# Grouped-query decode attention with a small MLP on one core: another place for the turn of p and for the loads of wo

## The chip, the cores and the metric

The kernel runs on one core of a Trainium2 chip. It is one program with five instruction streams: PE (TensorE, matrix products), DVE (VectorE), ACT (ScalarE), POOL (GpSimd) and SP (SyncE, which issues nearly all loads). The metric is the device time of one execution in microseconds. Lower is better.

## The reference

One token is decoded. Its normalised activations `xn` go through two blocks whose results are added to the input. Block A is attention of 32 query heads over 4 cached key/value heads of 65,536 positions. Block B is a small MLP.

```python
B, Sq, D = 1, 1, 1024
Hq, Hkv, Sk, Dh = 32, 4, 65536, 128          # everything in bfloat16

xn = layernorm(A_x)
# A
q = (xn @ wq).reshape(B, Sq, Hq, Dh).transpose(0, 2, 1, 3)
k = repeat(k_cache, 8, axis=1); v = repeat(v_cache, 8, axis=1)
p = softmax(einsum("bhqd,bhkd->bhqk", q, k) * Dh ** -0.5)
o = einsum("bhqk,bhkd->bhqd", p, v)
A = o.transpose(0, 2, 1, 3).reshape(B, Sq, Hq * Dh) @ wo      # wo: 4096 x 1024
# B (a fixed shift of column groups stands between w1 and w2; with one token it leaves zeros)
x1 = xn + shift(gelu(layernorm(xn) @ w1)) @ w2
Bm = x1 + gelu(layernorm(x1) @ w3) @ w4                       # w3: 1024 x 3584
out = A_x + A + Bm
```

Keys and values are 67 MB each, the weights 36 MB together; all are read once.

## The kernel before

**Order by hand.** Each engine has a queue object (`_Q`) to which the Python program appends instructions, and waits on semaphores where a buffer (`_B`) was last written or read by another engine. Every engine runs its queue strictly in the order in which the program appended it. Two lists set this order. `loads` is the order in which SP issues loads. `uses` is the order in which the loaded pieces are consumed; each use appends its instructions to PE, DVE and ACT. After each use `issue()` appends as many further loads as the ring has room for.

**The ring.** `slots_sb` has 8 slots of 16 KB in each of 128 partitions, so 2 MB each. Loads of keys, of values, of wq, w3 and the first one of w4 take an aligned pair of slots (`load2`, up to 4 MB); w1, w2, each quarter of wo and the last two of w4 take one slot (`load`, `load_pieces`). Slots are given out round robin. A load of a pair after a load of one slot skips the other slot of that pair (`room` rounds up to an even place). SP waits, load by load, until the earlier content of the slots has been read.

**Keys.** A head of 65,536 keys comes in four loads, and each load is used as two chunks (`use_k`, chunks `ch` 0 to 7 of a head). For a chunk DVE makes four 32x32-block transposes from the slot into `X` (line 512, two buffers by the chunk's parity), then takes the maximum of the scores of the chunk before (`max_k`, line 528), which ACT copies from PSUM to `S_sb` (line 529). PE makes the chunk's scores in 16 matmuls (line 521). So a key slot is free when DVE has transposed it.

**End of a head's keys.** `finish_head(h)` takes the maximum of the last chunk and of the head, and ACT makes the exponentials, four activations of 128 x 1024 elements into `p_sb` (line 539), with their sums in `lcol`.

**Turn of p.** `transpose_p(h)` turns `p_sb` into `pT_sb`: four times eight PE transposes (line 545) into one PSUM tile, and one ACT copy out of it (line 548). Each group of eight waits for the copy before.

**Values.** A value load is also used as two chunks (`use_v`, `n` 0 to 7), each 16 matmuls on PE against `pT_sb` into `OT_ps` (line 559). A value slot is free when PE has read it. After a head's last chunk `combine(h)` follows: ACT copies `OT_ps` (line 566), PE sums the parts (lines 567, 569), DVE divides and writes the head's eight columns of `oP_bf` (lines 572 to 576).

**wo.** `use_wo(h)` multiplies the head's quarter of wo by its columns of `oP_bf`, in 32 matmuls that accumulate into `M1_ps` with the MLP's parts (line 431, in `rows_mv`). Each matmul takes 32 columns as the stationary side, of which the first matters.

**Order around the change.** After the weights of the front come the four key loads of head 0. From then on a key load of head h and a value load of head h-1 alternate; the last four value loads have no keys between them. wo of head h-2 comes after the first value load while head h's keys run, wo of head 2 after the first of the last four value loads, wo of head 3 after the last. w4 closes the list. The turn of p of head h-1 is appended after the second chunk of head h; that of the last head stands before its first value chunk:

```python
                use_k(h, ch, ld)
                if ch == 1 and h > 0:
                    transpose_p(h - 1)
                if ch == NCH - 1:
                    finish_head(h)
```

Of the kernel before, what the change touches and what calls it, by code (L numbers as in the profile page):

```python
# [6 lines left out]
BF = mybir.dt.bfloat16  # L7
F32 = mybir.dt.float32
ACTF = mybir.ActivationFunctionType
ALU = mybir.AluOpType  # L10
# [85 lines left out]
def _op(q, fn, reads=(), writes=(), partial=False):  # L96
    _deps(q, reads, writes)
    ev = q.op(fn, True)
    _done(ev, reads, writes, partial)
    return ev  # L100
# [33 lines left out]
def bass_parallel_sum__gqa_block_cached__mixer_s_mlp__decode_kernel(  # L134
# [14 lines left out]
    P = 128  # L149
    D = A_x.shape[2]  # L150
    HKV, SK, DH = A_k_cache.shape[1], A_k_cache.shape[2], A_k_cache.shape[3]
# [4 lines left out]
    R = D // P  # L156
# [14 lines left out]
    with ExitStack() as es:  # L171
# [3 lines left out]
        def sb(name, shape, dt):  # L175
            return E(nc.sbuf_tensor(name, shape, dt))
# [4 lines left out]
        def sem(name):  # L181
            return E(nc.semaphore(name))
# [41 lines left out]
        cb_rL = sb("cb_rL", [P, 1], F32)  # L224
        cb_m = sb("cb_m", [P, 16, R], F32)
        cb_o = sb("cb_o", [P, R], F32)
        oP_bf = sb("oP_bf", [P, HKV * R + 32], BF)
        xr_bf = sb("xr_bf", [P, RW], BF)
        accr = sb("accr", [P, RW], F32)
        g_bf = sb("g_bf", [P, R + 32], BF)  # L230
# [15 lines left out]
        q_dve = _Q("dve", sem("c_dve"))  # L246
# [178 lines left out]
        def rows_mv(nkk, parts, st_fn, b_st, b_slot, b_out, first, last, k0=0):  # L425
            fns = []
            for kk in range(k0, k0 + nkk):
                for out_fn, mv_fn in parts:
                    for j in range(4):
                        fns.append(lambda e, kk=kk, j=j, out_fn=out_fn, mv_fn=mv_fn, st=(first and kk == k0), sp=(last and kk == k0 + nkk - 1):  # L430
                                   e.matmul(out_fn(j), st_fn(kk), mv_fn(kk, j), start=st, stop=sp, tile_position=(0, 32 * j), skip_group_check=True))  # L431
            _grp(q_pe, fns, reads=b_slot + [b_st], writes=b_out, partial=not first)
# [36 lines left out]
        def d_parts(view, c0):  # L469
            return [(lambda t: M1_ps[32 * t:32 * t + 32, c0:c0 + RW], lambda kk, t: view[:, kk * D + t * RW:kk * D + (t + 1) * RW])]  # L470
# [28 lines left out]

        def use_wo(h, ld):  # L500
            view, b = ld[0:2]
            rows_mv(R, d_parts(view, 0), lambda kk: oP_bf[:, h * R + kk:h * R + kk + 32], b_oP[h], b, [b_M1], False, False)

# [25 lines left out]
        def finish_head(h):  # L531
            max_k(NCH - 1)
            _op(q_dve, lambda e: e.reduce_max(mrow[:, 0:1], mcol[:, :], axis=AX.X), reads=[b_mcol], writes=[b_mrow])
            _op(q_dve, lambda e: e.tensor_tensor(out=Rm[:, :], in0=sel16[:, :], in1=mrow[:, 0:1].broadcast_to([P, 16]), op=ALU.mult),  # L534
                reads=[b_mrow, b_const], writes=[b_R])
            _op(q_pe, lambda e: e.matmul(M0_ps[:, 16:32], Lmat[:, :], Rm[:, :], start=True, stop=True), reads=[b_R, b_sel], writes=[b_M0])  # L536
            _op(q_dve, lambda e: e.tensor_reduce(out=brun[:, 0:1], in_=M0_ps[:, 16:32], axis=AX.X, op=ALU.min), reads=[b_M0], writes=[b_brun])
            for x in range(NB):
                _op(q_act, lambda e, x=x: e.activation(p_sb[:, :, :, :, x], S_sb[:, 2 * x:2 * x + 2, :].rearrange("p s (c i) -> p s c i", i=32),  # L539
                                                       ACTF.Exp, bias=brun[:, 0:1], scale=SCALE, accum_out=lcol[:, h % 2, x:x + 1]),  # L540
                    reads=[b_Ss[2 * x], b_Ss[2 * x + 1], b_brun], writes=[b_p, b_lcol[h % 2]], partial=x > 0)

        def transpose_p(h):
            for c8 in range(2 * CL // 8):
                _grp(q_pe, [lambda e, i=i, c=8 * c8 + i: e.transpose(out=PT_ps[:, i * P:(i + 1) * P],  # L545
                                                                    in_=p_sb[:, c // CL, c % CL, :, :].rearrange("p i h -> p (i h)"), identity=ident_bf[:])
                            for i in range(8)], reads=[b_p, b_const], writes=[b_PT])
                _op(q_act, lambda e, c8=c8: e.activation(pT_sb[:, :, 32 * c8:32 * c8 + 32, :].rearrange("p a x g -> p x a g"),  # L548
                                                         PT_ps[:, :].rearrange("p (x a g) -> p x a g", x=32, a=NA), ACTF.Copy),
                    reads=[b_PT], writes=[b_pT], partial=c8 > 0)  # L550
# [13 lines left out]
        def combine(h):  # L564
            _op(q_dve, lambda e: e.reduce_sum(Lacc[:, :], lcol[:, h % 2, :], axis=AX.X), reads=[b_lcol[h % 2]], writes=[b_Lacc])  # L565
            _op(q_act, lambda e: e.activation(O_acc[:, :], OT_ps[:, :], ACTF.Copy), reads=[b_OT], writes=[b_O])  # L566
            fns = [lambda e: e.matmul(M0_ps[:, 0:1], selL[:, :, :].rearrange("p g x -> p (g x)"), Lacc[:, :], start=True, stop=True)]  # L567
            for t in range(4):
                fns.append(lambda e, t=t: e.matmul(M0_ps[:, 256:384], selX[:, t, :, :].rearrange("p g x -> p (g x)"), O_acc[:, t * P:(t + 1) * P],  # L569
                                                   start=(t == 0), stop=(t == 3)))  # L570
            _grp(q_pe, fns, reads=[b_Lacc, b_O, b_sel], writes=[b_M0])
            _op(q_dve, lambda e: e.reciprocal(cb_rL[:, :], M0_ps[:, 0:1]), reads=[b_M0], writes=[b_cb])  # L572
            _op(q_dve, lambda e: e.tensor_tensor(out=cb_m[:, :, :], in0=M0_ps[:, 256:384].rearrange("p (x r) -> p x r", r=R),
                                                 in1=dmask[:, :].unsqueeze(2).broadcast_to([P, 16, R]), op=ALU.mult), reads=[b_M0, b_const], writes=[b_cb])
            _op(q_dve, lambda e: e.reduce_sum(cb_o[:, :], cb_m[:, :, :].rearrange("p x r -> p r x"), axis=AX.X), reads=[b_cb], writes=[b_cb])
            _op(q_dve, lambda e: e.tensor_scalar(out=oP_bf[:, h * R:(h + 1) * R], in0=cb_o[:, :], scalar1=cb_rL[:, 0:1], scalar2=None, op0=ALU.mult),
                reads=[b_cb], writes=[b_oP[h]])


        loads = [("wq", 0), ("wq", 1), ("w1",), ("w2",), ("w3", 0), ("w3", 1)]  # L580
        uses = [("wq", j) for j in range(4)] + [("w1",), ("w2",)] + [("w3", j) for j in range(4)]
        for h in range(HKV):
            for i in range(4):
                loads.append(("k", h, i))
                uses += [("k", h, 2 * i), ("k", h, 2 * i + 1)]
                if h > 0:
                    loads.append(("v", h - 1, i))
                    uses += [("v", h - 1, 2 * i), ("v", h - 1, 2 * i + 1)]
                if h > 1 and i == 0:
                    loads.append(("wo", h - 2))  # L590
                    uses.append(("wo", h - 2))
        for i in range(4):
            loads.append(("v", HKV - 1, i))
            uses += [("v", HKV - 1, 2 * i), ("v", HKV - 1, 2 * i + 1)]
            if i == 0:
                loads.append(("wo", HKV - 2))
                uses.append(("wo", HKV - 2))
        loads += [("wo", HKV - 1)] + [("w4", i) for i in (0, 2, 3)]
        uses += [("wo", HKV - 1)] + [("w4", i) for i in range(4)]

        layer_norm(xP, b_x, xn, xn_bf, b_xn, 0)
        _op(q_dve, lambda e: e.tensor_scalar(out=accr[:], in0=xr_bf[:], scalar1=ln_s[:, 1:2], scalar2=ln_s[:, 4:5], op0=ALU.add, op1=ALU.mult),
# [20 lines left out]
        for it in uses:  # L623
            ld = ready.pop(it)
            kind, args = it[0], it[1:]
            if kind == "wq":
                if args[0] == 3:
                    late_consts()
                    layer_norm(xn, b_xn, xn2, xn2_bf, b_xn2, 2)
                use_wq(args[0], ld)  # L630
            elif kind == "k":
                h, ch = args
                use_k(h, ch, ld)
                if ch == 1 and h > 0:
                    transpose_p(h - 1)
                if ch == NCH - 1:
                    finish_head(h)
            elif kind == "v":
                h, n = args
                if h == HKV - 1 and n == 0:  # L640
                    transpose_p(h)
                use_v(h, n, ld)
                if n == 2 * NA - 1:
                    combine(h)
            else:
                dict(w1=use_w1, w2=use_w2, w3=use_w3, wo=use_wo, w4=use_w4)[kind](*args, ld)
            for i in ([ld[2]] if it[0] != "w3" else [ld[2] // 2 * 2, ld[2] // 2 * 2 + 1]):
                taken[i] -= 1
            issue()
# [38 lines left out]
```

## Time and profile before

| | |
|---|---|
| Time, median of 3 runs | 409.18 us (407.23 to 410.07) |
| The profiled execution, its own time | 409.36 us |
| Its span, first to last instruction | 407.4 us |
| Busy: PE, DVE, ACT, POOL | 156.6, 187.8, 80.5, 7.5 us |
| Read from memory | 169.87 MB, 417 GB/s over the span |
| Mean granted PE clock | 0.618 of full |
| Key and value loads, median from issue to landing | 29.3 and 27.5 us |
| SP waits for DVE's key transposes | 186.4 us in 15 waits |
| SP waits for PE's value matmuls | 113.5 us in 15 waits |

The profile is one execution. Times are microseconds from the span's start. A timeline row shows start, duration, engine, line, operation, destination <- source, count, and in brackets how long the engine was idle before and what ended that. A row by stretch shows its bounds, its length, the busy time and the instruction count of PE, of PE's weight loads, of DVE, ACT and POOL, then PE's granted clock, the busy share of the 16 DMA engines, and GB/s. SP's long waits mean only that the ring is full; a load lands some 28 us after its issue since two or three others are ahead of it in the queue.

### The profile page before, as it was taken

What the parts mean: (1) busy time and instruction counts of PE and PEld (TensorE: products, weight loads), DVE (VectorE), ACT (ScalarE), POOL (GpSimd) and SP (SyncE); (2) the same over time, 40 slices, a digit from 0 to 9 for tenths busy, and PEclk for the clock granted to TensorE, in tenths of its full rate; (3) what the DMA queues carried; (4) which work ended last, traced back from release to release, by engine and by line L of the source; (5) the groups of instructions that cost most, each with busy time, mean ns of one, the idle gap of its engine ahead of it and who ended that gap; (6) DMA issues with size and microseconds to landing.
All of it is one profiled execution on the core that took longest, in us unless ns stands there. A gap on an engine that the chain in (4) does not pass through costs nothing.

```text
span 407.4 us, 3981 instructions
## 1 busy us (share of the span) xinstructions
PE 156.6 (38%) x1647; PEld 71.8 (18%) x1647; DVE 187.8 (46%) x264; ACT 80.5 (20%) x87; POOL 7.5 (2%) x38
## 2 busy tenths in 40 slices
PE   0273333333257050523470323325731515364445
PEld 0132111111023020102240111122410101231133
DVE  0255029999846364608481828054908183100010
ACT  1000000111861010390320101912300005630000
POOL 5000000000000000000000000000000000000000
PEclk9985655555567557565677565555575655569556
DMA  8999999999999999999999999999999999999994
GB/s 360 412 423 440 420 444 431 420 450 415 441 430 415 449 425 431 439 417 438 431 384 441 434 413 450 421 428 439 375 412 415 452 418 421 454 412 384 418 405 195
DMA packets 7377, 170.12 MB, mean 418 GB/s; under 512 B 952, under 2 KB 960, under 8 KB 1856
## 3 DMA queue, kind: packets, MB, share of 16 engines
q1 hardware_dynamic: 7208, 169.87, 97.7%
q8 instruction: 13, 0.21, 0.2%
q14 instruction: 4, 0.03, 0.0%
q10 hardware_dynamic: 152, 0.00, 0.0%
HBM read 169.87 MB, written 0.00 MB: 417 GB/s over the span
## 4 chain that ended last, share of the span: by engine, by line
DMA 68%; DVE 21%; PE 7%; issue 3%; SPq 1%; POOL 0%; ACTq 0%
DMA slots_sb<-in_A_k_cache_dram 51%; DVE X L512 18%; DMA slots_sb<-in_B_w_dram 7%; DMA slots_sb<-in_A_v_cache_dram 7%; DMA xr_bf<-in_A_x_dram 3%; PE OT_ps L559 3%; DVE mcol L528 2%; PE S_ps L431 2%; PE S_ps L521 1%; SPq L310 1%; PE M_ps L407 0%; PE M_ps L415 0%; PE M_ps L536 0%; POOL ln_s L419 0%; DVE Rm L534 0%
## 5 line engine op out<-in xcount | busy, mean ns | idle before, releaser
L512 DVE STREAM_TRANSPOSE X<-slots_sb 128x1024 f32<-128x1024 f32 x128 | 147.2, 1209 | 79.2 <-DMA slots_sb<-in_A_k_cache_dram 79.2
L521 PE MATMUL S_ps<-X,Yall 128*32 128x512 bf16 x512 | 56.1, 582 | 147.2 <-DVE X L512 147.2
L529 ACT ACTIVATE S_sb<-S_ps 128x512 f32<-128x512 f32 x32 | 19.2, 599 | 206.9 <-DVE mcol L528 206.9
L559 PE MATMUL OT_ps<-slots_sb,pT_sb 128*32 128x512 bf16 x512 | 47.3, 533 | 16.2 <-DMA slots_sb<-in_A_v_cache_dram 11.4
L521 PEld LDWEIGHTS S_ps<-X,Yall 128*32 128x32 bf16 x512 | 16.4, 121 | 181.9 <-DVE X L512 167.0
L539 ACT ACTIVATE p_sb<-S_sb,brun 128x1024 bf16<-128x1024 f32 x16 | 41.6, 2597 | 1.9 <-DVE Lacc L565 0.8
L572 DVE RECIPROCAL cb_rL<-M_ps 128x1 f32<-128x1 f32 x4 | 0.7, 168 | 73.9 <-PE M_ps L569 73.9
L559 PEld LDWEIGHTS OT_ps<-slots_sb,pT_sb 128*32 128x32 bf16 x512 | 17.8, 125 | 39.4 <-issue 22.8
L528 DVE TENSOR_REDUCE mcol<-S_ps 128x1 f32<-128x512 f32 x32 | 21.1, 658 | 7.1 <-PE S_ps L521 7.1
L548 ACT ACTIVATE pT_sb<-PT_ps 128x1024 bf16<-128x1024 bf16 x16 | 16.4, 1024 | 19.2 <-PE PT_ps L545 19.2
L545 PE MATMUL PT_ps<-ident_bf,p_sb 128*128 128x128 bf16 x128 | 14.1, 277 | 13.4 <-ACT pT_sb L548 13.4
L431 PE MATMUL S_ps<-slots_sb,xn_bf 128*32 128x512 bf16 (+1 forms) x128 | 12.7, 570 | 10.6 <-DMA slots_sb<-in_B_w_dram 9.2
L545 PEld LDWEIGHTS PT_ps<-ident_bf,p_sb 128*128 128x128 bf16 x128 | 10.6, 126 | 18.6 <-ACT pT_sb L548 16.0
L567 PE MATMUL M_ps<-Lacc,selL 128*128 128x1 f32 x8 | 2.2, 348 | 24.6 <-ACT O_acc L566 24.6
L443 ACT ACTIVATE ge_a<-ge_b 128x8 f32<-128x8 f32 (+1 forms) x2 | 0.4, 216 | 52.2 <-DVE ge_b L442 52.2
L435 DVE STREAM_TRANSPOSE X<-S_ps 128x512 f32<-128x512 f32 (+1 forms) x3 | 2.5, 847 | 14.3 <-PE S_ps L431 14.2
L431 PE MATMUL M_ps<-slots_sb,gh_bf 128*32 128x256 bf16 x112 | 5.9, 365 | 6.7 <-DMA slots_sb<-in_B_w_dram 6.7
L569 PE MATMUL M_ps<-O_acc,selX 128*128 128x128 f32 x32 | 8.2, 438 | 0.0
L431 PEld LDWEIGHTS S_ps<-slots_sb,xn_bf 128*32 128x32 bf16 x128 | 4.3, 133 | 17.0 <-DMA slots_sb<-in_B_w_dram 10.0
L569 PEld LDWEIGHTS M_ps<-O_acc,selX 128*128 128x128 f32 x32 | 7.3, 333 | 0.0
L651 DVE TENSOR_TENSOR fin<-accr,M_ps 128x256 bf16<-128x256 f32 x1 | 0.4, 422 | 14.6 <-PE M_ps L431 14.6
L566 ACT ACTIVATE O_acc<-OT_ps 128x512 f32<-128x512 f32 x4 | 2.5, 619 | 23.3 <-PE OT_ps L559 23.3
(90 smaller groups left out, 64.7 us busy)
## 6 DMA issues: line engine op xcount, KB each, us to landing
slots_sb<-in_A_k_cache_dram SPq DMA_DIRECT2D x16, 4096.0 KB, 29.3
slots_sb<-in_A_v_cache_dram SPq DMA_DIRECT2D x16, 4096.0 KB, 27.5
slots_sb<-in_A_wq_dram SPq DMA_DIRECT2D x2, 4096.0 KB, 16.7
slots_sb<-in_A_wo_dram SPq DMA_DIRECT2D x4, 2048.0 KB, 29.4
slots_sb<-in_B_w_dram SPq DMA_DIRECT2D x2, 3584.0 KB, 33.6
slots_sb<-in_B_w_dram SPq DMA_DIRECT2D x2, 2048.0 KB, 28.0
slots_sb<-in_B_w_dram SPq DMA_DIRECT2D x1, 4096.0 KB, 27.8
slots_sb<-in_B_w_dram SPq DMA_DIRECT2D x5, 512.0 KB, 27.2
```

Of the source, the lines that this page charges most:

```text
L310: ev = q_sp.dma(lambda e, dst=dst, src=src: e.dma_start(out=dst, in_=src), ch.sem, 16 * ch.n)
L431: e.matmul(out_fn(j), st_fn(kk), mv_fn(kk, j), start=st, stop=sp, tile_position=(0, 32 * j), skip_group_check=True))
L435: _op(q_dve, lambda e: e.transpose(out=X32[:, 1, c0:c0 + 32 * n], in_=src), reads=b_src, writes=[b_X[1][0]], partial=c0 > 0)
L512: _op(q_dve, lambda e, ix=ix: e.transpose(out=X32[:, m, 1024 * ix:1024 * (ix + 1)], in_=K32[:, 1024 * ix:1024 * (ix + 1)]), reads=b, write ...
L521: fns.append(lambda e, we=we, c_mid=c_mid, mv=mv: e.matmul(S_ps[bank][32 * c_mid:32 * c_mid + 32, :], Yall[:, h, we, :, :].rearrange("p a ...
L528: _op(q_dve, lambda e: e.reduce_max(mcol[:, ch:ch + 1], S_ps[bank][:, :], axis=AX.X), reads=[b_S[bank]], writes=[b_mcol], partial=ch > 0)
L529: _op(q_act, lambda e: e.activation(S_sb[:, ch, :], S_ps[bank][:, :], ACTF.Copy), reads=[b_S[bank], b_mcol], writes=[b_Ss[ch]])
L539: _op(q_act, lambda e, x=x: e.activation(p_sb[:, :, :, :, x], S_sb[:, 2 * x:2 * x + 2, :].rearrange("p s (c i) -> p s c i", i=32), ACTF.Ex ...
L545: _grp(q_pe, [lambda e, i=i, c=8 * c8 + i: e.transpose(out=PT_ps[:, i * P:(i + 1) * P], in_=p_sb[:, c // CL, c % CL, :, :].rearrange("p i ...
L548: _op(q_act, lambda e, c8=c8: e.activation(pT_sb[:, :, 32 * c8:32 * c8 + 32, :].rearrange("p a x g -> p x a g"), PT_ps[:, :].rearrange("p ...
L559: fns.append(lambda e, cl=cl, q4=q4, x0=x0: e.matmul(OT_ps[32 * q4:32 * q4 + 32, :], pT_sb[:, a, x0:x0 + 4, :].rearrange("p x g -> p (x g) ...
L569: fns.append(lambda e, t=t: e.matmul(M0_ps[:, 256:384], selX[:, t, :, :].rearrange("p g x -> p (g x)"), O_acc[:, t * P:(t + 1) * P], start ...
```

## The change

The two lists are built from one loop with a lag of five loads between keys and values, and wo is loaded in two pairs: wo of heads 0 and 1 after value load 8 (counted over all heads), wo of heads 2 and 3 after value load 15. The turn of p of heads 1 to 3 is appended directly after `combine` of the head in front; that of head 0 stays after the second chunk of head 1. `oP_bf` gets 32 spare columns for each head instead of 32 behind the last.

```diff
-        oP_bf = sb("oP_bf", [P, HKV * R + 32], BF)
+        oP_bf = sb("oP_bf", [P, HKV, R + 32], BF)
...
-            rows_mv(R, d_parts(view, 0), lambda kk: oP_bf[:, h * R + kk:h * R + kk + 32], b_oP[h], b, [b_M1], False, False)
+            rows_mv(R, d_parts(view, 0), lambda kk: oP_bf[:, h, kk:kk + 32], b_oP[h], b, [b_M1], False, False)
...
-            _op(q_dve, lambda e: e.tensor_scalar(out=oP_bf[:, h * R:(h + 1) * R], in0=cb_o[:, :], scalar1=cb_rL[:, 0:1], scalar2=None, op0=ALU.mult),
+            _op(q_dve, lambda e: e.tensor_scalar(out=oP_bf[:, h, 0:R], in0=cb_o[:, :], scalar1=cb_rL[:, 0:1], scalar2=None, op0=ALU.mult),
...
-        for h in range(HKV):
-            for i in range(4):
-                loads.append(("k", h, i))
-                uses += [("k", h, 2 * i), ("k", h, 2 * i + 1)]
-                if h > 0:
-                    loads.append(("v", h - 1, i))
-                    uses += [("v", h - 1, 2 * i), ("v", h - 1, 2 * i + 1)]
-                if h > 1 and i == 0:
-                    loads.append(("wo", h - 2))
-                    uses.append(("wo", h - 2))
-        for i in range(4):
-            loads.append(("v", HKV - 1, i))
-            uses += [("v", HKV - 1, 2 * i), ("v", HKV - 1, 2 * i + 1)]
-            if i == 0:
-                loads.append(("wo", HKV - 2))
-                uses.append(("wo", HKV - 2))
-        loads += [("wo", HKV - 1)] + [("w4", i) for i in (0, 2, 3)]
-        uses += [("wo", HKV - 1)] + [("w4", i) for i in range(4)]
+        LAG = 5
+        order = [("k", i) for i in range(LAG)]
+        for i in range(LAG, 4 * HKV):
+            order += [("v", i - LAG), ("k", i)]
+        order += [("v", i) for i in range(4 * HKV - LAG, 4 * HKV)]
+        for kind, i in order:
+            h, j = divmod(i, 4)
+            loads.append((kind, h, j))
+            uses += [(kind, h, 2 * j), (kind, h, 2 * j + 1)]
+            if kind == "v" and i in (8, 15):
+                for n in ((0, 1) if i == 8 else (2, 3)):
+                    loads.append(("wo", n))
+                    uses.append(("wo", n))
+        loads += [("w4", i) for i in (0, 2, 3)]
+        uses += [("w4", i) for i in range(4)]
...
                 use_k(h, ch, ld)
-                if ch == 1 and h > 0:
-                    transpose_p(h - 1)
                 if ch == NCH - 1:
                     finish_head(h)
+                if h == 1 and ch == 1:
+                    transpose_p(0)
             elif kind == "v":
                 h, n = args
-                if h == HKV - 1 and n == 0:
-                    transpose_p(h)
                 use_v(h, n, ld)
                 if n == 2 * NA - 1:
                     combine(h)
+                    if h < HKV - 1:
+                        transpose_p(h + 1)
```

## The prediction

> **What bounds the kernel now.** I read the page first, then transfer rates by stretch, then the timeline from 155 to 405 us. Loads are numbered through all heads, K0 to K15 and V0 to V15, 4 MB each. From the page:
>
> ```profile
> q1 hardware_dynamic: 7208, 169.87, 97.7%
> ...
> L572 DVE RECIPROCAL cb_rL<-M_ps 128x1 f32<-128x1 f32 x4 | 0.7, 168 | 73.9 <-PE M_ps L569 73.9
> ```
>
> The load queue is busy 97.7% of the span and the busiest engine, DVE, 46%: the loads are the bound, and only time in which the queue lacks work can be won. In the second line DVE idles 73.9 us before the four reciprocals of `combine`; that costs time only where it lets the queue run dry. Rates by stretch (last columns: PE's granted clock, DMA share, GB/s):
>
> ```profile
> 20.00:200.00 180.00, 68.99 (x676) 28.03 (x668) 107.41 (x159) 36.71 (x41) 1.10 (x2) 0.59 1.00 430
> 200.00:220.00 20.00, 10.22 (x147) 5.50 (x144) 10.30 (x10) 4.27 (x5) 0.00 (x0) 0.81 0.96 407
> 220.00:284.00 64.00, 21.85 (x185) 9.18 (x185) 32.55 (x38) 15.43 (x16) 0.00 (x0) 0.53 1.01 433
> 284.00:304.00 20.00, 11.05 (x149) 6.23 (x147) 10.42 (x10) 4.27 (x5) 0.00 (x0) 0.67 0.94 391
> 304.00:360.00 56.00, 19.24 (x163) 8.68 (x163) 22.99 (x30) 16.57 (x17) 0.00 (x0) 0.56 1.00 432
> 360.00:380.00 20.00, 9.11 (x136) 4.64 (x136) 0.00 (x0) 1.40 (x2) 0.00 (x0) 0.76 0.95 388
> ```
>
> Fed, the queue moves 431 GB/s (mean of the three long stretches). The three short ones fall behind: 20 x (24 + 40 + 43) / 431 = 5.0 us. These are the holes. The timeline shows the first two:
>
> ```profile
> 185.19 0.17 DVE L572 RECIPROCAL cb_rL<-M_ps 128x1 f32<-128x1 f32 x1 [13.68 <-PE M_ps L569]
> 186.27 9.12 DVE L512 STREAM_TRANSPOSE X<-slots_sb 128x1024 f32<-128x1024 f32 x8
> 195.48 0.33 SPq L295 DMA_DIRECT2D slots_sb<-in_A_v_cache_dram  x1
> 205.23 3.60 PE L559 MATMUL OT_ps<-slots_sb,pT_sb 128*32 128x512 bf16 x32 [1.21 <-ACT pT_sb L548]
> 208.93 0.33 SPq L295 DMA_DIRECT2D slots_sb<-in_A_k_cache_dram  x1
> 222.47 4.62 DVE L512 STREAM_TRANSPOSE X<-slots_sb 128x1024 f32<-128x1024 f32 x4 [10.25 <-DMA slots_sb<-in_A_k_cache_dram]
> 241.90 4.62 DVE L512 STREAM_TRANSPOSE X<-slots_sb 128x1024 f32<-128x1024 f32 x4 [9.13 <-DMA slots_sb<-in_A_k_cache_dram]
> ```
> ```profile
> 285.66 4.62 DVE L512 STREAM_TRANSPOSE X<-slots_sb 128x1024 f32<-128x1024 f32 x4 [5.72 <-DMA slots_sb<-in_A_k_cache_dram]
> 293.73 0.33 SPq L295 DMA_DIRECT2D slots_sb<-in_A_k_cache_dram  x1
> 306.65 4.62 DVE L512 STREAM_TRANSPOSE X<-slots_sb 128x1024 f32<-128x1024 f32 x4 [10.08 <-DMA slots_sb<-in_A_k_cache_dram]
> ```
>
> V5 is issued at 195.48, when DVE has read K8. K10 needs V4's slots; PE reads V4 at 205.23 to 208.83, after turning p, and SP issues K10 at 208.93, too late. The price stands in the landings, since DVE starts on keys the moment they land: K10 (222.47) to K11 (241.90) is 19.43 for two loads, 9.72 each; K9 (DVE starts on it at 201.92) to K10 is 20.55, so 1.12 were lost. The same at K14: K13 (285.66) to K14 is 20.99, so 1.56 lost. The third hole is V15's, issued at 366.73 when V12 has been read: PE starts on V14 at 371.41 and on V15 at 382.13, 10.72 for one load, 1.00 lost. Sum 3.68 us. It is less than 5.0 because the rate is a mean of 16 DMA engines and a landing is that of the last; the end of the kernel follows landings, so I take 3.7 and keep 5.0 as the upper end.
>
> **The change, part by part.** *Order of keys and values.* Written out, both lists read K0 to K4, V0, K5, V1, K6 and so on to K15, V11, V12 to V15. Nothing changes: cost 0, one answer. Only wo moves.
>
> *wo in pairs.* Before, each wo load takes one slot, and the next 4 MB load skips the other: for its time in the ring three pairs of slots hold data and one is half empty. wo0 follows V4 and wo1 V8, just where the head's end holds up the slots. After, wo0 and wo1 fill one pair behind V8, wo2 and wo3 one behind V15. Same bytes, same four DMAs. Around the first hole wo0's 2 MB (4.9 us at 431 GB/s) leave the queue, and every load inherits another slot: K9 takes K7's, V5 takes V3's (free at 174.8, when PE has read V3; SP issued K9 then), K10 takes K8's (free at 195.4), V6 takes V4's. K9 plus V5 are now in the queue long before K8 is read. K10's data must start when V5 has landed: before, at 222.47 - 1.12 - 9.72 = 211.6, so after at 211.6 - 4.9 = 206.7. It is issued at 195.5; allowing 2 us from issue to data (after 293.73 the rate recovers within that), 9 us are spare.
>
> *p turned behind the last values of the head in front.* For heads 1 and 2 the 32 transposes and four evictions come directly after `combine`, ahead of K8's and K12's score matmuls. One turn takes 281.34 to 290.03, 8.7 us at half clock (4 x (1.03 to 1.04 PE + 1.02 ACT + hand-overs)). It waits for p, whose last exponential ends at 182.1, and `combine`'s matmuls already wait for ACT behind that and end at 185.15: no new wait for p. Queued behind the turn on PE are K8's 32 matmuls, and DVE's maxima wait for those. The turn runs 185.2 to 193.9. K8's first scores, ready at 191.0, go 193.9 to 195.8 and its second, ready at 195.5, to 197.7; DVE's first maximum waits 0.5 us past 195.31, covered by the 5.95 us in which DVE waits for K9 at 201.92. DVE reads K8 whole before that maximum, so K8's slots come free at 195.4 as before. On ACT the evictions stand before copies of scores not yet made. V4 then runs 197.7 to 201.4 instead of 205.2 to 208.8, and V6, which inherits its slots, needs data only at 216.4: 13 us spare. Uncovered, the turn would cost 8.7 us a head; its cover is those spares. Head 0's turn stays (only the order of two ifs changes), and head 3's follows `combine(2)` directly before and after.
>
> *Heads 2 to 3.* The same: V9 waits for DVE's reading of K12 (279.45 before, some 6 us earlier after, since wo0 is no longer ahead of it and the first hole is gone), needed when K13 lands at about 284.5: 9 us spare. K14 waits for V8, V10 for wo1's use, each needed over 10 us later. The holes of 1.12 and 1.56 go.
>
> *Tail.* V15 now inherits V11's slots, free at 344.6, not V12's: its 1.00 goes. wo2 and wo3 wait for V12 (about 364 after); V15 lands at about 382.1 - 3.7 - 4.9 = 373.5, so with 2 us to start they have 7.5 us spare, the smallest of all. PE uses wo2 behind `combine(3)`: 3.6 us of V15's matmuls and some 5 of combining, while wo2, wo3 and 4 MB of w4 (19.5 us) still come. Behind w4 the order is as before: the end follows its last piece. SP still issues ten DMAs in a row here, and the rate is 336 from 368 to 372 and 393 from 372 to 376; if the burst itself slows the queue, the 1.00 may stay: lower end 2.7.
>
> *oP_bf.* 160 columns instead of 64 to clear on POOL: its memset of 64 columns took 0.14 us and that of 512 (permWE) 0.51, so +0.1, hidden because POOL's constants end near 7 us and x arrives at 15.2. Uncovered 0.1.
>
> **Two rules against the rows.** Full rate: 169.87 MB at 431 GB/s are 394.1 us of the 407.4. The Trainium skill ("DMA: Bandwidth & Descriptors", Where 436 GB/s comes from) puts the ceiling at 435 GB/s; by that figure alone the bytes take 390.3 us, an estimate, and the row stands 1% short of it, so no order of loads makes the fed queue faster. PE clock: turned at full clock eight transposes took 0.62 us (199.52), at half clock 1.03 (197.37). The skill ("TensorE: Matmul & The Clock Gate", What's actually happening) says that the array falls to half clock after an idle window of about 3.4 us; it speaks against the new place, behind some 8 us in which PE waited for ACT, and an estimate from the two rows is 4 x 0.41 = 1.6 us more on a turn. I use 8.7, the half-clock turn, so the sum is the same by the rule and by the row.
>
> **Sum.** Span 407.4 - 3.7 = 403.7. The profiled execution took 409.36, 1.96 around its span: 405.7. It lay 0.18 above the median of 409.18: 405.5 predicted.
>
> **The rivals.** *A, holes filled* (0.55): 405.5, its own range 404.2 (gain 5.0) to 406.5 (gain 2.7), with 0.8 us either way for the spread of runs (407.23 to 410.07). *B, more than the landings show* (0.19): the mean rate counts, 5.0, and K14 to K15's 1.56 (306.65 to 327.64 is 20.99 again, with K15 issued 32 us ahead, so no slot caused it) also goes: 409.2 - 6.6 = 402.6. Against it: nothing in the change touches that load. *C, holes only move* (0.19): the queue runs dry at another load, or wo's and w4's burst slows it, and 1 to 2 us are won: 407.7. For it: 388 GB/s beside the tail's burst; against it: spares of 7 us and up. *D, slower* (0.07): the turn stands in the keys' way. If K8's and K12's slots were free only after the turn (8.7 later) and one more chunk on DVE (5.1, for a full X), K10 would be issued at 195.5 + 13.8 = 209.3, its data 4.6 us late, twice: 9.2 lost, 3.7 won, 414.7. It decides from 9 us of delay; DVE's program order, reading both chunks before it waits, speaks against it.
>
> **Chances.** A change of 1% (4.1 us: below 405.1 or above 413.3) is about what can be told from none. A lies just above that border, so I put 0.22 of it on faster and 0.33 on same; B is faster, C same; D slower. Faster 0.41, same 0.52, slower 0.07. The range leaves out D, the half of B beyond its centre and the slow end of C: 402.6 to 408.6.
>
> **What will show it.** Rates of 428 and over in every 20 us stretch from 20 to 380; keys landing 19.4 apart throughout; V5, K10, V6 issued at least 7 us before the load ahead lands; on PE the 32 transposes between `combine` and K8's scores. Wrong: a stretch under 420 between 190 and 300 (D or C), or a full queue at a lower rate.

## The result, and the profile after

The changed kernel takes 405.28 us (median of 6 runs, 405.25 to 405.43), the kernel before beside it 409.62 (6 runs, 407.23 to 410.27). The ratio is 0.9905, 95% interval 0.9878 to 0.9931: 0.7 to 1.2% faster. The median is 0.2 us from the forecast. The profiled execution took 405.26 with a span of 403.3, where 403.7 was forecast. The spread of the runs fell too, from 3.0 to 0.2 us.

Page of the kernel after, the same two lines as before:

```profile
q1 hardware_dynamic: 7208, 169.87, 98.4%
...
L572 DVE RECIPROCAL cb_rL<-M_ps 128x1 f32<-128x1 f32 x4 | 0.7, 168 | 68.3 <-PE M_ps L569 68.3
```

DVE still idles nearly as long before the reciprocals; the load queue's share rose. The rates by stretch (last column GB/s):

```profile
20.00:200.00 180.00, 72.92 (x724) 31.65 (x716) 110.53 (x162) 39.87 (x44) 1.10 (x2) 0.59 1.00 430
200.00:220.00 20.00, 6.76 (x64) 2.43 (x64) 10.87 (x12) 1.20 (x2) 0.00 (x0) 0.61 1.00 431
220.00:284.00 64.00, 27.38 (x299) 13.96 (x299) 29.01 (x35) 18.54 (x19) 0.00 (x0) 0.63 1.00 430
284.00:304.00 20.00, 6.85 (x64) 2.47 (x64) 10.30 (x10) 1.20 (x2) 0.00 (x0) 0.59 1.00 433
304.00:360.00 56.00, 21.04 (x171) 10.05 (x171) 23.00 (x30) 17.81 (x18) 0.00 (x0) 0.56 1.00 432
360.00:380.00 20.00, 13.76 (x142) 6.77 (x146) 0.00 (x0) 0.60 (x1) 0.00 (x0) 0.67 0.99 422
```

The stretches that stood at 407, 391 and 388 stand at 431, 433 and 422. Timeline of the kernel after, around the former first hole:

```profile
184.82 1.06 PE L545 MATMUL PT_ps<-ident_bf,p_sb 128*128 128x128 bf16 x8
...
186.15 9.12 DVE L512 STREAM_TRANSPOSE X<-slots_sb 128x1024 f32<-128x1024 f32 x8
...
192.26 1.90 PE L521 MATMUL S_ps<-X,Yall 128*32 128x512 bf16 x16
...
195.36 0.33 SPq L295 DMA_DIRECT2D slots_sb<-in_A_k_cache_dram  x1
...
196.36 1.93 PE L559 MATMUL OT_ps<-slots_sb,pT_sb 128*32 128x512 bf16 x32
197.03 4.62 DVE L512 STREAM_TRANSPOSE X<-slots_sb 128x1024 f32<-128x1024 f32 x4 [1.18 <-DMA slots_sb<-in_A_k_cache_dram]
198.38 0.33 SPq L295 DMA_DIRECT2D slots_sb<-in_A_v_cache_dram  x1
...
216.47 4.62 DVE L512 STREAM_TRANSPOSE X<-slots_sb 128x1024 f32<-128x1024 f32 x4 [9.13 <-DMA slots_sb<-in_A_k_cache_dram]
```

The turn begins directly behind `combine`, in PE's former wait for DVE's transposes. K10 goes out when K8 has been read (195.36, before 208.93), V6 when V4 has been read (198.38), and K9 (197.03) to K10 (216.47) is 19.44. Further on:

```profile
285.59 4.62 DVE L512 STREAM_TRANSPOSE X<-slots_sb 128x1024 f32<-128x1024 f32 x4 [11.61 <-DMA slots_sb<-in_A_k_cache_dram]
...
305.02 4.62 DVE L512 STREAM_TRANSPOSE X<-slots_sb 128x1024 f32<-128x1024 f32 x4 [9.13 <-DMA slots_sb<-in_A_k_cache_dram]
...
324.44 4.62 DVE L512 STREAM_TRANSPOSE X<-slots_sb 128x1024 f32<-128x1024 f32 x4 [9.12 <-DMA slots_sb<-in_A_k_cache_dram]
...
362.47 1.60 SPq L286 DMA_DIRECT2D slots_sb<-in_A_wo_dram  x2
...
373.10 3.61 PE L559 MATMUL OT_ps<-slots_sb,pT_sb 128*32 128x512 bf16 x32 [5.35 <-DMA slots_sb<-in_A_v_cache_dram]
```

K13 to K14 is 19.43 (before 20.99), K14 to K15 19.42 (before 20.99), and wo2 and wo3 are issued at 362.5, over 10 us before V15 lands at 373.1. Two details differ from the forecast: K13 lands when it did before (285.59 against 285.66), though the first hole is gone; and K15's unexplained 1.56 is gone too. Both come up again below, with the instruction loads.

### The profile page after: what moved, and what is told of

Read it like the earlier page. It is cut to its first block, busy times and chain, and to the rows that moved or that the text cites. A ratio compares the mean times of both kernels' runs of the same rounds, so it can differ in the third digit from the quotient of the medians.

```text
span 403.3 us, 3981 instructions
## 1 busy us (share of the span) xinstructions
PE 159.8 (40%) x1647; PEld 74.1 (18%) x1647; DVE 187.9 (47%) x264; ACT 80.5 (20%) x87; POOL 7.6 (2%) x38
## 4 chain that ended last, share of the span: by engine, by line
DMA 64%; DVE 21%; PE 7%; ACT 4%; issue 3%; SPq 1%; POOL 0%; ACTq 0%
DMA slots_sb<-in_A_k_cache_dram 53%; DVE X L512 18%; DMA slots_sb<-in_B_w_dram 8%; DMA xr_bf<-in_A_x_dram 3%; ACT p_sb L539 3%; PE OT_ps L559 3%; DVE mcol L528 2%; PE S_ps L431 1%; ACT pT_sb L548 1%; PE PT_ps L545 1%; PE S_ps L521 1%; SPq L310 1%; PE M_ps L569 0%; PE M_ps L415 0%; PE M_ps L407 0%
## 5 line engine op out<-in xcount | busy, mean ns | idle before, releaser
L521 PE MATMUL S_ps<-X,Yall 128*32 128x512 bf16 x512 | 58.3, 601 | 142.3 <-DVE X L512 142.3
L559 PEld LDWEIGHTS OT_ps<-slots_sb,pT_sb 128*32 128x32 bf16 x512 | 19.5, 130 | 32.4 <-issue 23.4
L545 PE MATMUL PT_ps<-ident_bf,p_sb 128*128 128x128 bf16 x128 | 16.6, 311 | 13.4 <-ACT pT_sb L548 13.4
L545 PEld LDWEIGHTS PT_ps<-ident_bf,p_sb 128*128 128x128 bf16 x128 | 12.9, 143 | 17.6 <-ACT pT_sb L548 16.6
L567 PE MATMUL M_ps<-Lacc,selL 128*128 128x1 f32 x8 | 2.2, 347 | 25.4 <-ACT O_acc L566 25.4
L567 PEld LDWEIGHTS M_ps<-Lacc,selL 128*128 128x128 f32 x8 | 2.0, 309 | 28.2 <-issue 28.2
```

Of the source, the lines that this page charges most:

```text
L521: fns.append(lambda e, we=we, c_mid=c_mid, mv=mv: e.matmul(S_ps[bank][32 * c_mid:32 * c_mid + 32, :], Yall[:, h, we, :, :].rearrange("p a ...
L559: fns.append(lambda e, cl=cl, q4=q4, x0=x0: e.matmul(OT_ps[32 * q4:32 * q4 + 32, :], pT_sb[:, a, x0:x0 + 4, :].rearrange("p x g -> p (x g) ...
```

## The experiments

In the shared comparisons of the first four experiments the kernel before has a median of 408.35 (17 runs, 407.05 to 410.52), in the next four 408.63 (12 runs), in the last two 408.44 (11 runs).

**Which part does it?** First the turn alone:

```diff
+                if h == 1 and ch == 1:
+                    transpose_p(0)
...
                     combine(h)
+                    if h < HKV - 1:
+                        transpose_p(h + 1)
```

> The kernel before with the turn of p at its new place and wo where it was (and the new layout of oP_bf). Theory: the values of heads 1 and 2 are read some 8 us earlier, so K10 and K14 are issued in time and the first two holes (1.12 and 1.56 us) go; V15 still waits for V12, so the third (1.00) stays: 2.7 us less than before, 406.5 to 406.9. Rival 1, the pairs of wo do everything and the turn nothing: 409.2 to 409.6. Rival 2, the turn stands in the keys' way: more than 413.

Measured: 405.34 us (405.20 to 406.67; ratio 0.9930, 0.9903 to 0.9958). That is the level of the changed kernel, 405.28, with the third hole still open. By the ratio it is 2.9 us less than the kernel before (1.7 to 4.0), and 2.7 lies within that. The 406.5 to 406.9 were missed also because they start from 409.2 to 409.6, where the kernel before took 408.35 in this comparison. The first two stretches are full now; V15 is as late as foretold, and its stretch is short of rate. Rows by stretch, SP and the value matmuls of this kernel:

```profile
200.00:220.00 20.00, 7.21 (x64) 2.48 (x64) 10.30 (x10) 1.20 (x2) 0.00 (x0) 0.66 1.00 431
...
284.00:304.00 20.00, 7.03 (x64) 2.48 (x64) 10.30 (x10) 1.20 (x2) 0.00 (x0) 0.71 1.00 430
...
360.00:380.00 20.00, 10.29 (x148) 4.87 (x152) 0.00 (x0) 0.00 (x0) 0.00 (x0) 0.76 0.97 409
```
```profile
364.10 0.33 SPq L295 DMA_DIRECT2D slots_sb<-in_A_v_cache_dram  x1
```
```profile
368.39 1.91 PE L559 MATMUL OT_ps<-slots_sb,pT_sb 128*32 128x512 bf16 x32 [1.87 <-DMA slots_sb<-in_A_v_cache_dram]
...
378.12 2.32 PE L559 MATMUL OT_ps<-slots_sb,pT_sb 128*32 128x512 bf16 x20 [7.82 <-DMA slots_sb<-in_A_v_cache_dram]
```

The changed kernel has 422 in the last of these stretches without a hole, so the rate of 409 says that the hole takes 20 x 13 / 431 = 0.6 us on the mean of the DMA engines. Yet V14 (368.39) to V15 (378.12) is 9.73, a full-speed load. The trace shows why. It holds 16 landing records for each load, which I read as one for each of the 16 DMA engines; PE and DVE start on a load when the last has come. The first and the last of the 16, in us, for V14, V15 and the last piece of w4 (the numbers are those of the profiled executions; `h3_x2` and `few_mm` come further below):

| Kernel | V14 | V15 | Last piece of w4 |
|---|---|---|---|
| before | 368.59, 371.37 | 378.90, 382.09 | 401.36, 404.35 |
| changed | 359.93, 363.27 | 369.63, 373.06 | 396.88, 400.25 |
| the turn alone (`turn_only`) | 364.83, 368.35 | 375.86, 378.08 | 398.20, 400.37 |
| the turn alone, that of head 3 twice (`h3_x2`) | 365.03, 368.40 | 384.40, 386.14 | 406.71, 408.45 |
| changed, fewer matmuls (`few_mm`) | 360.03, 362.36 | 369.74, 372.07 | 396.99, 399.26 |

With the turn alone the first landing of V15 comes 11.03 us after that of V14, the last 9.73 after. The hole idles the DMA engines that are ahead, and the one that lands last, which the kernel waits for, loses nothing. At the end the first landing is 1.3 us later than in the changed kernel, the mean of the 16 is 0.5 later (399.05 against 398.54), the last 0.1, and the time differs by 0.06.

Then the pairs of wo alone, the two ifs of the turn put back:

> The changed kernel with the turn of p at its old place, so wo in pairs alone. Theory: every load inherits slots that come free earlier (K10 those of K8 and V15 those of V11) and all three holes go without the turn: 405.3, the same as the changed kernel within 0.5 us. Rival 1, the turn is what fills the first two holes: only the third goes, 408.3 to 408.6.

Measured: 405.26 (405.15 to 405.41; ratio 0.9921, 0.9898 to 0.9945), as the theory has it. So each part fills the first two holes by itself. The two halves of the reorder of wo, each on the kernel before with the new layout of `oP_bf`:

```diff
-            if i == 0:
-                loads.append(("wo", HKV - 2))
-                uses.append(("wo", HKV - 2))
-        loads += [("wo", HKV - 1)] + [("w4", i) for i in (0, 2, 3)]
...
+        for n in (2, 3):
+            loads.append(("wo", n))
+            uses.append(("wo", n))
```

> The kernel before with wo2 moved behind V15, beside wo3; wo0, wo1 and the turn of p as before. Theory: only the third hole goes, V15 landing 9.7 us behind V14: 1.0 us less than before, 408.3 to 408.6, with K10 and K14 still late. Rival, the burst of ten issues at the tail slows the queue whatever V15 waits for: no change, 409.3 to 409.6.

Measured: 407.92 (406.91 to 408.93, 12 runs; ratio 0.9981, 0.9963 to 1.0), so 0.8 us, between 0 and 1.5 (0.4 by the medians): it agrees with the 1.0 but hardly excludes zero. The new layout of `oP_bf`, which this kernel has and which was not run alone, is part of this 0.8 at most. The profile is in no doubt about the places: two holes stand, one is filled.

```profile
200.00:220.00 20.00, 11.35 (x149) 6.67 (x146) 10.42 (x10) 4.27 (x5) 0.00 (x0) 0.67 0.96 401
284.00:304.00 20.00, 12.29 (x152) 7.09 (x152) 10.42 (x10) 4.27 (x5) 0.00 (x0) 0.67 0.94 392
360.00:380.00 20.00, 12.48 (x136) 5.27 (x136) 0.00 (x0) 2.27 (x3) 0.00 (x0) 0.67 0.99 425
```

This kernel also explains K15. K14 (306.22) to K15 (327.16) is 20.94 here, where the second hole stands, as it was 20.99 before; it is 19.42 in the turn alone and 19.50 in the next kernel, both with the second hole filled. By the landing records the 16 engines land K14 within 0.4 us of each other, since the hole lets those behind catch up. Then one of them lands K15 1.55 late and the other 15 on time, while an instruction load (16 KB of program, on the second queue of the page) runs from 320.3. In the turn alone one engine is late at K15 as well, but the engines are 3.3 us apart there, and it still lands no later than the last (324.36 and 324.37). So K15's 1.56 comes with the second hole in both profiles that have it, and counts to its price.

```diff
-                if h > 1 and i == 0:
-                    loads.append(("wo", h - 2))
-                    uses.append(("wo", h - 2))
+                if h == 3 and i == 0:
+                    for n in (0, 1):
+                        loads.append(("wo", n))
+                        uses.append(("wo", n))
```

> The kernel before with wo0 and wo1 as a pair behind V8; wo2, wo3 and the turn of p as before. Theory: the first two holes go, the third stays: 2.7 us less than before, 406.5 to 406.9, the same as with the turn alone, since either is enough for these two holes. Rival, the gains of the turn and of the pair add up and each fills half: 408.0 to 408.3.

Measured: 405.30 (405.18 to 405.59; ratio 0.9923, 0.9900 to 0.9947). Redundant with the turn, as expected. It is 3.1 us by the ratio (2.2 to 4.1), which again holds the 2.7; the level is again that of the changed kernel, though V15 still waits for V12 and its stretch stands at 408.

**How far is the turn from hurting?** On the changed kernel, with 2 and with 4:

```diff
                     if h < HKV - 1:
-                        transpose_p(h + 1)
+                        for _ in range(2 if h < 2 else 1):
+                            transpose_p(h + 1)
```

> The changed kernel with the turns of p of heads 1 and 2 made twice in a row (the second overwrites pT_sb with the same values), 8.6 us more on PE ahead of K8's and K12's scores. Theory: the turn lies in the spare of the ring (V6's data is needed at 216.5, V4 is then read by about 209): no change, 405.3 within 0.5 us. Rival, the turn stands in the keys' way and costs what it takes: 8 us a head, 415 or more.

Measured: 405.30 (405.18 to 405.44). Two more turns, 17 us more in PE's queue, cost nothing.

> The same with these two turns made four times, 25.8 us more each. Theory: now beyond the spare: V4 is read at about 225.5, V6's data comes at 227.4 where V5 and K10 have landed by 216.5, a hole of 10.9 us, and one of about 10 at K14: 426, far less than the 51.6 us that PE has more. Rival, the cost grows in step with the turns: 457.

Measured: 425.49 (425.22 to 425.76), 20.2 more, where 20.7 were expected. Rows by stretch of this kernel at the two places:

```profile
214.00:225.00 11.00, 7.30 (x80) 3.49 (x80) 5.04 (x5) 3.49 (x4) 0.00 (x0) 0.66 0.21 63
...
304.00:314.00 10.00, 8.71 (x143) 4.76 (x141) 5.26 (x6) 2.65 (x3) 0.00 (x0) 0.69 0.20 54
```

The queue all but stops (63 and 54 GB/s), twice, until a late load is issued: V6 at 223.42, when PE has read V4, and K14 at 312.18, when PE has read V8. So a turn that is long enough does cost time, and the point where it does lies beyond one extra turn. It is not the way of rival D of the prediction: K8's slots came free in time (K10 was issued at 195.32); the slots of the values came late.

**What does a hole cost?** The third hole made deep, on the kernel with the turn alone: the turn of head 3 twice (`range(2 if h == 2 else 1)`).

> The kernel with the turn alone (wo where it was before), the turn of head 3 made twice, so that V12 is read 8.6 us later and V15, which takes its slots, is issued 8.6 us later, at about 372.5. Theory A, the end follows the last of the 16 DMA engines, and a hole costs only what that engine idles: it lands V14 at 368.4, V15's data starts at about 374.2, 5.8 us: 411.1. Theory B, a hole costs what the queue idles on the mean, and the 1 us of mean rate lost at V15 in the kernel with the turn alone was made good elsewhere: all 8.6 us, 413.9.

Measured: 413.47 (413.02 to 414.13), 8.1 more than the turn alone: neither number, nearer to B, whose 413.9 lies in the spread of the runs. The timeline of SP and of PE's value matmuls:

```profile
372.71 0.33 SPq L295 DMA_DIRECT2D slots_sb<-in_A_v_cache_dram  x1
```
```profile
386.19 3.23 PE L559 MATMUL OT_ps<-slots_sb,pT_sb 128*32 128x512 bf16 x32 [9.64 <-DMA slots_sb<-in_A_v_cache_dram]
```

V15, issued into an empty queue at 372.71, is used 13.48 us later, not 1.7 + 9.72 as theory A had assumed. Its first packets start at 373.70, 1.0 us after the issue. By the landing records 15 of its 16 parts land 11.7 to 12.3 us after the issue and the last 13.4; an instruction load of 0.88 us runs from 378.16. The two restarts of an empty queue in the kernel with four turns also end 13.4 us after the issue (V6 at 236.82, K14 at 325.56). K10 and K14 of the kernel before look alike (13.54 and 12.92 from issue to use), but there the load ahead was still landing for 2.7 and 1.6 us after the issue.

This run does not decide between the theories. At the end of the kernel the last landing is 8.08 us later than with the turn alone, the mean of the 16 is 8.15 later: a deep hole costs both the same. With the longer restart A gives the 8.1 that were measured, but the restart was read from this same run. What decides is the shallow hole above, where the mean was 0.5 us late at the end, the last landing 0.1 and the time 0.06.

**Is the queue now all that counts?** Without the loads and products of w1 and w2 (the latter's is a product with zeros, since one token leaves nothing after the shift):

```diff
-        loads = [("wq", 0), ("wq", 1), ("w1",), ("w2",), ("w3", 0), ("w3", 1)]
+        loads = [("wq", 0), ("wq", 1), ("w3", 0), ("w3", 1)]
...
+                    _op(q_dve, lambda e: e.tensor_copy(x1[:], xn[:]), reads=[b_xn], writes=[b_x1])
```

> The changed kernel without the loads and products of w1 and w2. The product with w2 is that of zeros (with one token the shift between w1 and w2 leaves nothing), so x1 is copied from xn. 4.19 MB less. Theory: the queue is never dry, so the time falls by what they take at 431 GB/s, 9.7 us: 395.5. Rival, with the holes gone something else is next (DVE or PE at the head's ends, the front's chain): 398 or more.

Measured: 395.38 (395.36 to 395.57; ratio 0.9672, 0.9641 to 0.9702): 9.9 less than the changed kernel for 9.7 expected. This is the fastest version here that gives the reference's result, and it beats both kernels, by leaving bytes out and not by order.

The other way round, PE's work taken away and all loads kept: one of four score matmuls and four of sixteen value matmuls.

```diff
-            for we in range(4):
+            for we in range(1):
...
-            for cl in range(CL):
+            for cl in range(4):
```

> The changed kernel with one of the four score matmuls of each part and four of the sixteen value matmuls of each chunk (three quarters of both products are left out; all loads stay). 1,536 PE instructions fewer, so fewer instruction loads on the second queue of the page (13 of 16 KB in every kernel of this length): about 7. Theory: with the queue never dry the end is set by the DMA engine that lands last, which is behind the others because instruction loads fall on it: 1 to 2 us less, 403.3 to 404.3. Rival, the engines differ by themselves or PE's work matters not at all: 405.3 within 0.3.

Measured: 404.01 (403.90 to 404.18), 1.3 less. On its page the queue of instruction loads, 13 before and after:

```profile
q8 instruction: 7, 0.11, 0.1%
```

And the rates of the last microseconds, the changed kernel first:

```profile
396.00:398.00 2.00, 1.04 (x32) 0.34 (x20) 0.00 (x0) 0.00 (x0) 0.00 (x0) 1.00 0.77 294
398.00:400.00 2.00, 0.98 (x20) 0.25 (x12) 0.00 (x0) 0.00 (x0) 0.00 (x0) 0.73 0.28 100
```
```profile
396.00:398.00 2.00, 1.14 (x20) 0.18 (x13) 0.00 (x0) 0.00 (x0) 0.00 (x0) 0.69 0.72 268
398.00:400.00 2.00, 0.99 (x16) 0.33 (x16) 0.35 (x1) 0.00 (x0) 0.00 (x0) 1.00 0.08 28
```

At 28% in the last two microseconds some DMA engines still work while the others are done; with fewer instruction loads that share is down to 8%, and the kernel ends 1.1 us earlier in span. The landing records say it engine by engine (the table above): the first engine ends where it did in the changed kernel (396.99 and 396.88), the last 1.0 us earlier (399.26 and 400.25). So the data take as long as before, and the engines that were behind are less far behind. In the changed kernel one such step can be seen alone: while an instruction load of 1.07 us runs from 281.1, the distance from first to last landing grows from 2.3 to 3.35 us and stays there. That step is why K13 landed no earlier than before. The last landing accounts for 1.0 of the 1.3 us; that no other effect of the missing matmuls takes part is not shown.

Last, values six loads behind the keys:

```diff
-        LAG = 5
+        LAG = 6
```

> The changed kernel with the values six loads behind the keys instead of five. The copy of O_acc no longer stands behind the next head's exponentials for heads 0 to 2, so DVE's idle time before the reciprocals falls from 68.3 us to about 30. Theory: only the queue counts, and it is full already: 405.3 within 0.5. Rival, the waits of DVE and PE at the head's ends still cost something: 403 or less.

Measured: 405.05 (404.99 to 405.23), 0.2 less. The line of the reciprocals on its page:

```profile
L572 DVE RECIPROCAL cb_rL<-M_ps 128x1 f32<-128x1 f32 x4 | 0.7, 168 | 62.6 <-PE M_ps L569 62.6
```

The wait did not fall to 30 us; its cause changed. PE waits 3.9 us for ACT's copies of `OT_ps` (25.4 in the changed kernel), but ACT itself waits 33.0 us (16.8) for the value matmuls before them. So this run does not test what the wait costs; it shows only that another lag brings next to nothing.

## Why the prediction was right, point by point

- *The loads are the bound.* Shown: 10 us of bytes less are 10 us less (no_w12), 17 us more in PE's queue are nothing (turn_x2). Up to the tail the fed queue stayed at 430 to 433 GB/s in both kernels.
- *Same order of keys and values.* Right by SP's issues: they differ in the places of wo alone.
- *The first two holes, 2.7 us.* The mechanism is right and each half of it suffices: K10 and K14 in time, by the turn (turn_only) or by the pair (wo01_only). With only these filled, the time falls by 2.9 and 3.1 us by the ratios (intervals 1.7 to 4.0 and 2.2 to 4.1): 2.7 lies in both, and the time is the same 405.3 as with all three. The 2.7 leaves out K15's 1.56, which went with the second hole, so what each hole is worth is less well known than the sum.
- *The third hole, 1.00, added to them.* This term of the sum failed. Filled alone it brings 0.8 (0 to 1.5); after the other two it brings nothing (405.34 without, 405.28 with). I read it off the landings before and added it as a lack of work, though a hole costs only what the last DMA engine loses, and here that engine had work: V15 was issued at 366.73, some 4 us before its last part of V14 was read. With the turn alone, where V15 is as late, it loses 0.01 (V14 to V15 9.73). The 1.00 before (10.72) goes with slow packets: there 32 KB took 1.26 to 1.51 us on the mean of each 2 us from 368 to 376, and 1.22 to 1.24 in the turn alone from 366 to 374. Why they were slow stays open.
- *The number 405.5.* It is as near as it is partly by luck. It starts from 409.18, the median of three runs; in the 40 later runs the kernel before has medians of 408.35 to 408.63. From there to 405.28 is some 3.2 us, so the base was 0.7 too high and the gain of 3.7 some 0.5 too large, and the two errors cancel. By the ratio beside the changed kernel the gain is 3.9 (2.8 to 5.0), which holds both.
- *The split over time.* K13 was to land at 284.5 and landed at 285.59; K15 gained 3.2. The landings of the profile before held, besides the holes, a delay of one DMA engine beside an instruction load (K15's 1.56), and the profile after holds another (at K13, from 281.1). The argument against rival B, that nothing in the change touches K15's load, failed: the slip went with the second hole. B's own time, 402.6, was 2.7 us too low.
- *The turn in front of the keys.* Right: 184.82 to 193.4, 8.6 us where 8.7 were forecast, each group of eight transposes at half clock (1.03 to 1.06 us; granted clock 0.50 from 184.8 to 193.4), as the idle-window rule of the Trainium skill ("TensorE: Matmul & The Clock Gate", What's actually happening) has it for a PE that had waited some 8 us; V4 read even earlier than foretold (198.3 for 201.4), since PE by then had its full clock (granted 1.00 from 196.3 to 198.3). The 2 us allowed from issue to data were enough for the data to start (1.0 us in h3_x2), but the landing of a load into an empty queue comes 3.7 us later than its 9.72 at full speed. The spares were large enough.
- *Tail.* V15 at 373.1 (373.5 forecast), wo2 issued at 362.5 (364). The rate of 428 in every stretch was missed in the last, 422; the burst of issues stands there in both kernels, and whether it is the cause was not tried.

## What to carry to other kernels

Where the load queue is the bound, look in the rates by stretch for places where it falls short, find the issue that came late and which read it waited for, and free that slot earlier or give the load another slot: here either was enough, and doing both was not worth more. Price such a hole by the spacing of landings, but don't add holes up: the end follows the DMA engine that lands last, a shallow hole may idle only the others, and here filling two holes made the third free. Take the base from more than three runs when the gain looked for is 1%. Work on a compute engine that is moved in front of a consumer is free as long as the slots it holds back are due later than it ends; repeat it until the time moves, and you know how much room there is.

## What the runs showed of the hardware

- The kernels at 405.3 repeat within 0.2 to 0.4 us (changed kernel, wo_only, turn_x2, and wo01_only with its shallow third hole); the kernel before spreads over 3.5 us (407.05 to 410.52 in 17 runs). The turn alone, with its shallow third hole, had five runs at 405.2 to 405.5 and one at 406.67.
- The last part of 4 MB issued into an empty queue lands 13.4 us after the issue (V15 in h3_x2, V6 and K14 in turn_x4), where loads in a full queue follow each other at 9.72. In h3_x2 15 of the 16 parts landed by 12.3.
- Instruction loads hold up single DMA engines that carry the data: the engines end 3.4 us apart with 13 instruction loads (changed kernel, 405.28) and 2.3 apart with 7 (three quarters of the matmuls gone, 404.01), and the first of them ends at the same time.
- The kernel ends by the DMA engine that lands last: with the turn alone the first ends 1.3 us later than in the changed kernel, the last 0.1, and the time is 405.34 for 405.28.
